# Summing the second layer of a top-1 expert network in 128 columns, with its banks, logits and key loads rearranged

## The chip, the cores and the metric

The kernel runs on one core of a Trainium2 chip. The metric is the device time of one execution in microseconds. Before the change three runs took 819.81, 827.26 and 831.77 us; their median is 827.26 us.

The core has a tensor engine (PE; its weight loads have a row of their own, PEld), a vector engine (DVE), a scalar engine (ACT), a general engine (POOL) and a sync engine (SP) that issues most transfers. Each engine works off its own instructions in the order in which they were written. Products land in PSUM, which has eight banks of 512 f32 columns on 128 partitions.

## The reference

Inputs are q, k and v (4 batches of 11,456 tokens, 128 channels), 49 agents per batch, and the weights of 8 experts with 1,024 hidden units.

```python
def sm(a, b):
    s = scale * (a @ b.transpose(0, 2, 1))
    s = s - s.max(-1, keepdims=True)
    e = np.exp(s)
    return e / (e.sum(-1, keepdims=True) + 1e-09)
a2k = sm(agents, k);  agent_v = a2k @ v
x = sm(q, agents) @ agent_v                       # 45,824 tokens of 128 channels
...
logits = x @ w_gate                               # 8 experts, the best one is taken
gate_w = softmax(logits)[best];  eom = 1 / (1 + exp(-(x @ w_output_gate)))
...
h = np.maximum(x[mask] @ w1[e], 0.0)              # for each expert e
out[mask] = gate_w[mask, None] * eom[mask, e, None] * (h @ w2[e])
```

## The kernel before

Every token is a mix of 49 agent averages, so the kernel keeps for each token the 49 exponentials of its scores instead of x. In f16 these stand three times in one row of 128: the rounded value, the rest that rounding lost, and 30 of the rounded values again. A DMA turns such rows, so that `x1` has the 128 numbers on partitions and the tokens in columns. For each batch the agent averages are multiplied into the first expert layer; only hidden units whose sign is not fixed for all tokens of the batch are kept (256 slots, `NBM` = 2 blocks of 128), and the others are added as one linear map `G`. Almost all tokens of a batch choose one expert; the tokens that do not ("left" tokens) are gathered and done again in 20 tiles with weights of their own.

The work of a batch, by the names of the code:

- **Keys and values.** `k_unit` and `v_unit` go over 12 units of 1,024 tokens (the last has 192). They give the agent averages. `folded` (line 869) then picks the expert, loads its two weight matrices and builds the first-layer weights `w` and `wr` (products `ha`, `hr`), the check weights `wc` (`hk`), the second-layer weights `vv` (`hv`) and the linear map `G` (`hg`). `wr` holds the 19 rows that did not fit into the 128 of `w`.
- **Queries.** `q_unit` and `q_rest` (line 1254) make scores, exponentials, the three-part f16 rows `e16`, the turned copy `x1`, a copy `x2` of its first 32 rows on partitions 32 to 63, then logits (`lg`) and the gate `smt`. `check` multiplies `x1` by `wc` (`ck`).
- **Tiles.** 92 tiles of up to 512 tokens. `mm1` (line 1443) makes the two blocks of the first layer in two banks: per block one product over 128 rows and one over the 19 rows of `wr`, block 0 from `x1` and block 1 from `x2`. `relu` writes the rounded `hh` on ACT and the rest `hl` on DVE. `mm2` (line 1476) makes the second layer for two groups of 128 tokens at a time, 256 columns each: `G` and then, for each block, `hh` times both halves of `vv` (256 columns) and `hl` times the first half. `finish` (line 1504) adds the two halves (ACT copies one, DVE adds the other), and `store` multiplies by the gate on POOL and stores.

**Banks.** `group` gives `mm1` of an even tile banks 0 and 1 and of an odd tile banks 2 and 3. The four others serve everything else: the halves of `y`, `ck`, `lg`, scores, averages and the fold.

**The order.** Nothing is scheduled by hand. A planner (`Clock`, `tick`, `block`, `idle`) runs while the program is written: it has a cost for each instruction (`Engine.cost`) and lets a waiting stream go on when its operands should be ready. `main_stream` (line 1548) chooses between `mm1` of the next tile and `mm2` of the oldest open tile. So a changed cost or rule moves instructions on every engine. All products below bear line 229, the line that emits an instruction.

**Left tiles.** They go in sets of 4, 4, 4, 3 (batches 0 and 1) and 3, 2 (batches 2 and 3). A set is prepared (`tbs`, `pbs`, gathers) only when the results of the set before the last one are stored; a tile then needs `let`, `lx`, 8 products `lh` and 8 products `ly` in f32 (two rows each in a trace).

Of the kernel before, what the change touches and what calls it, by code (L numbers as in the profile page):

```python
# [17 lines left out]
P = 128  # L18
# [14 lines left out]
YS = 2  # L33
# [10 lines left out]
G4 = 4  # L44
# [117 lines left out]
class Engine:  # L162
# [16 lines left out]
    def cost(self, op, ins, outs, k):  # L179
        n = _free(outs[0])  # L180
        if self.name == "PE":
            wide = ins[0].dtype == F32
            if op == "transpose":
                return 110.0 if wide else 58.0
            if not wide and ins[0].shape[0] <= 32:
                return n / 4.8 + 51.0
            if wide and _free(ins[0]) <= 64 and ins[0].shape[0] > 64 and n <= P:

                return max(58.0, n * 0.833 + 4.0) * min(1.0, _free(ins[0]) / 64.0 * 0.8)
            if wide and not self.clk.started and n <= P:  # L190
                return 221.0
            return max(157.0, n * 1.667 + 6.0) if wide else max(n, 50) / 2.4 + 2.5
        if "reduce" in op:
            n = _free(ins[0])
        if self.name == "ACT":
            return (51.0 if ins[0].name in self.clk.psum else 93.0) + n / 1.2 + 93.0 * (len(ins) - 1)
# [82 lines left out]
def agent_attention_top1_moe(ctx, tc, qT, kT, v, aT, wg, wo, w1, w2, cst, sides, slots, out):  # L279
# [53 lines left out]
    def group(i):  # L333
        return [NBM * (i % 2) + g for g in range(NBM)]
# [272 lines left out]
    def loads():  # L607
        for n, item in enumerate(ITEMS):
            while n >= FIRST_ITEMS and (picking[0] or not X1):
                yield None  # L610
# [3 lines left out]
            if n == 1:  # L614
                load_constants()

# [27 lines left out]

    def k_unit(b, u):
        if u == 0:
            K[b] = dict(
# [6 lines left out]
        spawn(k_rest(b, u, s, mark))  # L654
# [214 lines left out]
    def folded(b, ad):  # L869

        w1t, w2t = yield from choose(b, ad[:, 0:A], ad)
# [113 lines left out]
    def hidden(b, ad, w1t, w2t):  # L985
# [83 lines left out]
        for n in range(NB):  # L1069
            for k in range(NBM):  # L1070
                PE.matmul(o[32 * k:32 * k + 32, 0:P], ax[:, n, P:P + 32], sel[:, n, k * P:(k + 1) * P],
                          start=(n == 0), stop=(n == NB - 1))
        clk.vt["PE"] += TURN
        rest = wk.tile([P, P], F16, name=f"wr{b}", tag="w0")
        yield from DVE.q.tensor_copy(rest[0:32 * NBM], o[0:32 * NBM, 0:P])
# [165 lines left out]
    def q_unit(b, u):  # L1241
        s, mark = yield from scores(("q", b, u), f"qs{b}_{u}")
        spawn(q_rest(b, u, s, mark))

    rests = []

# [7 lines left out]
    def q_rest(b, u, s, mark):  # L1254
# [3 lines left out]
        while me > 3 and rests[me - 4] < 3 or me > 1 and not state.get(0, {}).get("w"):  # L1258
# [4 lines left out]
        z = wk.tile([P, 8, A2], F32, name=f"qz{b}_{u}", tag="qz", bufs=2)  # L1263
        yield from DVE.q.tensor_tensor(z[0:pp, 0:nt, 0:A], sv,
                          m[0:pp, 0:nt].unsqueeze(2).broadcast_to([pp, nt, A]), op=ALU.subtract)
        release(mark)
        ef = wk.tile([P, 8, A2], F32, name=f"ef{b}_{u}", tag="ef", bufs=5)
        ev = ef[0:pp, 0:nt, 0:A]
        yield from ACT.q.activation(ev, z[0:pp, 0:nt, 0:A], AF.Exp, scale=SCALE)
        yield from ACT.q.activation(z[0:pp, 0:nt, 0:A], ev, AF.Square)  # L1270
        while counted[0] < b - 1:
            yield None
        rank_, e2, d256 = (marks[b % 2][0][0:pp, k, 8 * u:8 * u + nt] for k in range(3))
        yield from DVE.q.tensor_reduce(e2, z[0:pp, 0:nt, 0:A], axis=AX.X, op=ALU.add)
# [3 lines left out]
        yield from POOL.q.tensor_copy(e16[0:pp, 0:nt, 2 * A:P], ev[:, :, AR:A])  # L1278
        while me > 0 and rests[me - 1] < 1:
# [6 lines left out]
        while vacant_turned() is None:  # L1286
            yield None
        x2 = place(("x2", b, u), vacant_turned()[1], [1024], F16)
        yield from SY.q.dma_start(x2[32:64, 0:nt * pp], x1[0:32, 0:nt * pp])
        X1[b, u] = x1, x2  # L1290
        spawn(check(b, u, x1), 1)
        rests[me] = 1
        while "gs" not in state.get(b, {}) or (me > 0 and rests[me - 1] < 2) \
                or me > 2 and rests[me - 3] < 3:
            yield None
        gs, s3 = state[b]["gs"], state[b]["s3"]
# [7 lines left out]
        def tl(nm, *sh):  # L1304
            return wk.tile([P, 8, *sh], F32, name=f"{nm}{b}_{u}", tag=nm, bufs=3)[0:pp, 0:nt]

        lv = lg[0:pp, 0:nt * 36].rearrange("p (t a) -> p t a", a=36)
        L = tl("lL", 16)
        yield from ACT.q.copy(L, lv[:, :, 18:34])
        yield from DVE.q.tensor_scalar(d256, lv[:, :, 16], 1e-9, None, op0=ALU.add)  # L1310
        yield from DVE.q.tensor_tensor(L, lv[:, :, 0:16], L, op=ALU.add)
        release(mark)
        rests[me] = 2
        while not clk.started:
            yield None
        rr = tl("rr")
        yield from DVE.q.tensor_scalar(rr, d256, s3[0:pp], None, op0=ALU.mult)
        yield from DVE.q.reciprocal(rr, rr)
        l = tl("ll", 16)
        yield from POOL.q.tensor_tensor(l, L, rr.unsqueeze(2).broadcast_to([pp, nt, 16]), op=ALU.mult)  # L1320
# [41 lines left out]
    def q_tail(b):  # L1362

        st = state[b]
        while "thr" not in st or not all((b, u) in checked for u in range(NU)):
# [46 lines left out]

    PRE = 6
    QU = 6

    MIX0 = [(2, 0)] + [(1, 0)] * 4 + [(0, 0)] + [(0, 2)] * 6
    MIX = [(3, 0)] * 4 + [(0, 0)] + [(0, 2)] * 6 + [(0, 0)]
# [6 lines left out]
    def small_products():  # L1424
        for kind, b, u in ITEMS:
            while kind == "q" and not roomy(NU * b + u, AHEAD):
# [14 lines left out]
    done, summed = set(), set()  # L1441

    def mm1(i):
# [4 lines left out]
        x1, x2 = (x[:, 512 * h:512 * h + w] for x in X1[b, u])  # L1448
# [13 lines left out]
        if 4 * h + n == UNITS[u][2]:  # L1462
            scored(("x2", b, u))
# [12 lines left out]
    def mm2(i, k, f):  # L1476
# [4 lines left out]
        if f == 0:  # L1481
            Y[i, k] = bank(f"y{i}_{k}"), hold()
            x1 = X1[b, u][0]
            for j in range(2):
                sl = slice(512 * h + (2 * k + j) * pp, 512 * h + (2 * k + j + 1) * pp)
                PE.matmul(Y[i, k][0][0:pp, j * 2 * C:(j + 1) * 2 * C], x1[:, sl], state[b]["G"].rearrange("p h c -> p (h c)"),
                          start=(j == 0), stop=False)
# [3 lines left out]
        for j in range(2):  # L1491
            y = Y[i, k][0][0:pp, j * 2 * C:(j + 1) * 2 * C]
            sl = slice((2 * k + j) * pp, (2 * k + j + 1) * pp)
            PE.matmul(y, hh[:, sl], vv[:, f].rearrange("p h c -> p (h c)"), start=False, stop=False)
            tick()
            PE.matmul(y[:, 0:C], hl[:, sl], vv[:, f, 0, :], start=False, stop=(f == NBM - 1 and j == 1))
            tick(0, 1)
        if f == NBM - 1:
            spawn(finish(i, k), 0)
            block()  # L1500

    OS = {}

    def finish(i, k):
        b, u, h, pp, n = tiles[i]
        if k == 0:
            while i > 3 and i - 4 not in done or i > 1 and i - 2 not in summed:
                yield None
            OS[i] = wk.tile([P, 4, C], F32, name=f"os{i}", tag="os", bufs=4)
        os = OS[i]  # L1510
        y, mark = Y.pop((i, k))
        yv = y.rearrange("p (j h c) -> p j h c", h=2, c=C)
        ol = wk.tile([P, 2, C], F32, name=f"ys{i}_{k}", tag="ys", bufs=YS)
# [554 lines left out]
```

## Time and profile before

| | |
|---|---|
| median of three runs | 827.26 us |
| the profiled execution | 834.87 us |
| its span, first to last instruction | 833.1 us |
| busy PE, DVE, ACT, POOL | 668.7, 549.3, 466.7, 370.0 us |
| first tile's first product / last second-layer product | 71.4 / 698.3 us |
| mean granted clock of PE | 0.904 |

The profiled execution is 0.9% above the median. A busy PE is not PE at its peak: a product counts as busy until its results have left, while the next one has long begun. "idle before" in a group of instructions is the engine's idle time just before them, with what ended it.

### The profile page before, as it was taken

To read this page: it belongs to the slowest core of one execution; us is meant where nothing else is said; L and a number is where in the kernel's file an instruction comes from. 1 tells how busy PE (TensorE), PEld (TensorE's weight loads), DVE (VectorE), ACT (ScalarE), POOL (GpSimd) and SP (SyncE) were. 2 spreads that over 40 slices of the span, in tenths; PEclk is the share of its full clock that TensorE was granted. 3 is DMA by queue.
4 is the path that set the end of the run, shared out by engine and by line. 5 is a ranking of instruction groups with operands and counts; after the bars stand their busy time and mean duration, and the time that the engine had idled before them with its cause. 6 is when DMAs were issued, how large, how long until landed. Compare 5 with 4: busy or idle time off the path is not lost. (4 is left out here: it accounts for less than half of the span.)

```text
span 833.1 us, 28225 instructions
## 1 busy us (share of the span) xinstructions
PE 668.7 (80%) x11198; PEld 511.7 (61%) x11198; DVE 549.3 (66%) x1881; ACT 466.7 (56%) x1316; POOL 370.0 (44%) x622
## 2 busy tenths in 40 slices
PE   9989778877787889778888988867989797386484
PEld 7776645655555656556656666645666577285374
DVE  2966547658886777679679888697878666324220
ACT  2445547674747667675776676537777763131131
POOL 1012415855343386634235768444456643431330
PEclk9999959999979999989999899668999999695787
DMA  8993773878656986965759748644644455352440
GB/s 325 354 285 90 182 195 93 253 189 249 177 174 159 240 230 146 261 201 145 219 113 272 204 132 249 217 110 117 149 134 128 140 188 154 123 177 70 145 165 6
DMA packets 106185, 149.11 MB, mean 179 GB/s; under 512 B 61272, under 2 KB 69642, under 8 KB 106048
## 3 DMA queue, kind: packets, MB, share of 16 engines
q1 hardware_dynamic: 104128, 145.02, 60.2%
q0 software_dynamic: 1920, 2.24, 1.3%
q8 instruction: 89, 1.46, 0.8%
q14 instruction: 48, 0.39, 0.2%
HBM read 97.51 MB, written 35.56 MB: 160 GB/s over the span
## 5 line engine op out<-in xcount | busy, mean ns | idle before, releaser
L229 PE MATMUL y<-vv,hh 128*128 128x256 f16 x720 | 163.4, 285 | 1.7 <-issue 1.7
L229 PEld LDWEIGHTS <-x_ld 128*128 128x128 f16 x1080 | 90.5, 103 | 108.8 <-issue 76.2
L229 PE MATMUL y<-vv,hl 128*128 128x128 f16 x720 | 144.5, 226 | 1.5 <-issue 1.1
L229 DVE SCALAR_TENSOR_TENSOR hl<-h,hh 128x512 f16<-128x512 f32 (+1 forms) x184 | 118.1, 668 | 37.7 <-ACT hh L229 33.6
L229 ACT ACTIVATE hh<-h 128x512 f16<-128x512 f32 (+1 forms) x184 | 98.6, 583 | 49.5 <-PE h L229 45.0
L229 PE MATMUL y<-gw,x_ld 128*128 128x256 f16 x360 | 80.3, 285 | 54.1 <-ACT ck L229 25.7
L229 ACT ACTIVATE ck<-ck 128x512 f32<-128x512 f32 x180 | 106.0, 589 | 31.6 <-PE ck L229 22.8
L229 POOL TENSOR_TENSOR os<-os,smt 128x512 f32<-128x512 f32 (+1 forms) x91 | 94.4, 1041 | 43.5 <-DVE os L229 30.5
L229 ACT COPY ys<-y 128x256 f32<-128x256 f32 x179 | 66.2, 371 | 60.3 <-PE y L229 56.1
L229 DVE TENSOR_TENSOR os<-y,ys 128x256 f32<-128x256 f32 x179 | 74.3, 416 | 37.7 <-ACT ys L229 33.2
L229 PE MATMUL ck<-wc,x_ld 128*128 128x256 f16 x360 | 76.3, 294 | 17.8 <-ACT ck L229 7.8
L229 PEld LDWEIGHTS <-hh 128*128 128x128 f16 x720 | 74.4, 103 | 15.1 <-issue 5.9
L229 PEld LDWEIGHTS <-hl 128*128 128x128 f16 x720 | 75.4, 105 | 5.6 <-DVE hl L229 0.8
L229 POOL TENSOR_TENSOR e<-ef,e 128x392 f16<-128x392 f32 (+1 forms) x48 | 42.7, 890 | 53.7 <-ACT e L229 52.8
L229 PE MATMUL h<-x_ld,w 128*128 128x512 f16 (+1 forms) x184 | 64.2, 392 | 0.7 <-DVE hl L229 0.7
L229 PE MATMUL qs<-at,q_ld 128*32 128x50 f32 (+1 forms) x2640 | 46.5, 213 | 11.2 <-issue 10.0
L229 PEld LDWEIGHTS qs<-at,q_ld 128*32 128x32 f32 (+1 forms) x2640 | 38.5, 113 | 22.5 <-issue 16.0
L229 PE MATMUL ks<-at,k_ld 128*32 128x50 f32 (+1 forms) x2188 | 49.5, 217 | 2.3 <-issue 1.5
L229 PEld LDWEIGHTS ks<-at,k_ld 128*32 128x32 f32 (+1 forms) x2188 | 42.6, 121 | 11.1 <-issue 7.5
L229 POOL TENSOR_TENSOR ev<-S,km_o 128x400 f32<-128x400 f32 (+1 forms) x36 | 32.8, 913 | 27.0 <-PE av L229 26.2
L229 ACT ACTIVATE lh<-lh 128x512 f32<-128x512 f32 x40 | 23.9, 597 | 35.5 <-PE lh L229 34.3
L229 ACT COPY S<-ks 128x400 f32<-128x400 f32 (+1 forms) x48 | 22.6, 471 | 34.5 <-PE ks L229 34.0
(349 smaller groups left out, 1507.4 us busy)
## 6 DMA issues: line engine op xcount, KB each, us to landing
v_ld<-v SPq DMA_DIRECT2D x44, 512.0 KB
q_ld<-qT SPq DMA_DIRECT2D x44, 512.0 KB
out<-os SPq DMA_DIRECT2D x88, 256.0 KB
k_ld<-kT SPq DMA_DIRECT2D x43, 512.0 KB
lws<-w SPq DMA_DIRECT2D x22, 512.0 KB
lw<-w SPq DMA_DIRECT2D x18, 512.0 KB
efd<-ef SPq DMA_DIRECT2D x44, 200.0 KB
x_ld<-x_ld SPq DMA_DIRECT2D x44, 64.0 KB
```

The source lines that it names most:

```text
L229: return getattr(self.eng, op)(*a, **k)
```

## The change

- **Second layer.** `mm2` sums both halves of the weights into the same 128 columns: two products of 128 columns with the same stationary operand in place of one of 256, for `G` and for `hh`. Four groups of tokens share one bank, so a tile has one bank for `y`, where it had two. `finish` reads it once: DVE multiplies by the gate if the gate is there when the planner gets to it, else ACT copies and POOL multiplies.
- **First layer.** `group` gives every tile banks 0 and 1. The others are six (`G4` = 2). `wr` lies on partitions 0 to 18 for both blocks, and `x2` and its 48 transfers are gone.
- **Logits.** Two products of 18 columns into one sum, where one of 36 columns was followed by an ACT copy and a DVE addition. The multiplication by `rr` moves from POOL to DVE.
- **Queries.** `q_rest` is cut into streams (`q_weights`, `q_squares`, `q_logits`, `q_gates`); up to six units may be under way before the gates (`DEEP`), four behind them (`GATES`).
- **Keys and values.** Loads and products of q and of k and v are two streams each. A batch's keys may begin once the tiles have come to six units ahead of the batch before it (`LEAD`, `reached`), and the fold waits until the tiles have come to the batch before.
- The planner's costs of products over 32 rows and of ACT with a sum are changed.

```diff
-G4 = 4
+G4 = 2
...
             if not wide and ins[0].shape[0] <= 32:
-                return n / 4.8 + 51.0
+                return n / 2.4 + 51.0 if n <= 64 else n / 2.4 + 2.5
...
     def group(i):
-        return [NBM * (i % 2) + g for g in range(NBM)]
+        return [g for g in range(NBM)]
...
     def loads():
-        for n, item in enumerate(ITEMS):
-            while n >= FIRST_ITEMS and (picking[0] or not X1):
-                yield None
+        for n, item in enumerate(ITEMS[:FIRST_ITEMS]):
...
+        spawn(later_loads("q", 3), -1)
+        spawn(later_loads("kv", 4), -1)
...
     def k_unit(b, u):
         if u == 0:
+            while b > 0 and "rec" not in K[b - 1] or not reached(NU * (b - 1) + LEAD):
+                yield None
...
     def folded(b, ad):
 
+        while not reached(NU * (b - 1)):
+            yield None
...
-        while me > 3 and rests[me - 4] < 3 or me > 1 and not state.get(0, {}).get("w"):
+        while me >= DEEP and (rests[me - DEEP] < 3 or rests[me - 4] < 1) or me > 1 and not state.get(0, {}).get("w"):
...
         for t in range(nt):
-            yield from PE.q.matmul(lg[0:pp, t * 36:(t + 1) * 36], x1[:, t * pp:(t + 1) * pp],
-                                   gs.rearrange("p k c -> p (k c)"), start=True, stop=True)
+            for k in range(2):
+                yield from PE.q.matmul(lg[0:pp, t * 18:(t + 1) * 18], x1[:, t * pp:(t + 1) * pp], gs[:, k, :],
+                                       start=(t == 0 and k == 0), stop=(t == nt - 1 and k == 1))
...
         for g in range(NBM):
-            rows = slice(32 * g, 32 * g + AR)
-            PE.matmul(p[g][0][:, 0:w], rest[rows, :], (x2 if g else x1)[rows, :], start=False, stop=True)
+            PE.matmul(p[g][0][:, 0:w], rest[0:AR, g * P:(g + 1) * P], x1[0:AR], start=False, stop=True)
...
-        for j in range(2):
-            y = Y[i, k][0][0:pp, j * 2 * C:(j + 1) * 2 * C]
-            sl = slice((2 * k + j) * pp, (2 * k + j + 1) * pp)
-            PE.matmul(y, hh[:, sl], vv[:, f].rearrange("p h c -> p (h c)"), start=False, stop=False)
+        for j in range(2 * k, 2 * k + 2):
+            y = Y[i][0][0:pp, j * C:(j + 1) * C]
+            sl = slice(j * pp, (j + 1) * pp)
+            PE.matmul(y, hh[:, sl], vv[:, f, 0, :], start=False, stop=False)
+            PE.matmul(y, hh[:, sl], vv[:, f, 1, :], start=False, stop=False)
             tick()
-            PE.matmul(y[:, 0:C], hl[:, sl], vv[:, f, 0, :], start=False, stop=(f == NBM - 1 and j == 1))
+            PE.matmul(y, hl[:, sl], vv[:, f, 0, :], start=False, stop=(f == NBM - 1 and j == n - 1))
...
-        yield from ACT.q.copy(ol[0:pp], yv[0:pp, :, 1, :])
-        yield from DVE.q.tensor_tensor(os[0:pp, 2 * k:2 * k + 2, :], yv[0:pp, :, 0, :], ol[0:pp], op=ALU.add)
-        release(mark)
...
+        if (b, u) in SM and clk.ready[SM[b, u].name] <= max(clk.vt["DVE"], clk.now()):
+            yield from DVE.q.tensor_tensor(o, yv, gate(), op=ALU.mult)
+            release(mark)
+        else:
+            yield from ACT.q.copy(o, yv)
+            release(mark)
             while (b, u) not in SM:
                 yield None
+            yield from POOL.q.tensor_tensor(o, o, gate(), op=ALU.mult)
```

Of the 92 tiles of the changed program 72 take the ACT copy and 20 the DVE multiplication.

Three places on PE show how the order moves. The first is the start of the second layer of tile 40 (`y40`; `x11_8` is the turned copy of its unit, `gw_1` its linear map). Before:

```order
L229 LDWEIGHTS x11_8_ld_6802
L229 MATMUL y40_0_7432<-gw_1_85,x11_8_ld_6802 128x256
L229 LDWEIGHTS x11_8_ld_6802
L229 MATMUL y40_0_7432<-gw_1_85,x11_8_ld_6802 128x256
L229 LDWEIGHTS hh40_0_7284
L229 MATMUL y40_0_7432<-vv1_4829,hh40_0_7284 128x256
L229 LDWEIGHTS hl40_0_7285
L229 MATMUL y40_0_7432<-vv1_4829,hl40_0_7285 128x128
```

In the changed program the same tile's products of `hh` and `hl`, with a logit product among them:

```order
L229 LDWEIGHTS hh40_0_7989
L229 MATMUL y40_8100<-vv1_5194,hh40_0_7989 128x128
L229 LDWEIGHTS hh40_0_7989
L229 MATMUL y40_8100<-vv1_5194,hh40_0_7989 128x128
L229 LDWEIGHTS x11_9_ld_7471
L229 MATMUL lg1_9_7856<-gs_1_102,x11_9_ld_7471 128x18
L229 LDWEIGHTS hl40_0_7990
L229 MATMUL y40_8100<-vv1_5194,hl40_0_7990 128x128
```

The product of 256 columns has become two of 128, each with a weight load of its own.

The second place is the first product of the linear map of batch 3 (`hg3`), whose tiles begin with tile 69. Before:

```order
L229 LDWEIGHTS w3_11593
L229 MATMUL h72_1_11806<-x13_1_ld_11277,w3_11593 128x512
L229 LDWEIGHTS wr3_11629
L229 MATMUL h72_0_11802<-x13_1_ld_11277,wr3_11629 128x512
L229 LDWEIGHTS wr3_11629
L229 MATMUL h72_1_11806<-x23_1_ld_11350,wr3_11629 128x512
L229 MATMUL hg3_11820<-w2t3_11085,al3_11668 128x128 x3
```

In the changed program:

```order
L229 LDWEIGHTS wr2_7942
L229 MATMUL h66_1_11858<-x12_10_ld_11259,wr2_7942 128x512
L229 LDWEIGHTS x13_0_ld_11661
L229 MATMUL ck3_0_1_11853<-wc3_11730,x13_0_ld_11661 128x256
L229 LDWEIGHTS x13_0_ld_11661
L229 MATMUL ck3_0_1_11853<-wc3_11730,x13_0_ld_11661 128x256
L229 MATMUL qs3_2_11857<-at_76,q3_2_ld_11228 32x50 x32
L229 LDWEIGHTS x13_0_ld_11661
L229 MATMUL ck3_0_2_11913<-wc3_11730,x13_0_ld_11661 128x256
L229 LDWEIGHTS x13_0_ld_11661
L229 MATMUL ck3_0_2_11913<-wc3_11730,x13_0_ld_11661 128x256
L229 MATMUL hg3_11863<-w2t3_10642,al3_11742 128x128
```

It stood behind tile 72, the fourth tile of the new batch, and now stands behind tile 66, two tiles before the batch begins.

The third place is the table product of the third set of left tiles (`tbs0_8`); `y91` is the last tile. Before:

```order
L229 MATMUL y89_0_14007<-vv3_11559,hl89_1_13835 128x128
L229 LDWEIGHTS x13_10_ld_13455
L229 MATMUL y89_1_14036<-gw_1_85,x13_10_ld_13455 128x256
L229 MATMUL tbs0_8_14027<-big0_2_13966,ones_90 128x32
L229 LDWEIGHTS x13_10_ld_13455
L229 MATMUL y89_1_14036<-gw_1_85,x13_10_ld_13455 128x256
```

In the changed program:

```order
L229 LDWEIGHTS hl91_1_14626
L229 MATMUL y91_14748<-vv3_11538,hl91_1_14626 96x128
L229 MATMUL let0_4_14771<-kc_71,big0_1_13059 98x128
L229 MATMUL tbs0_8_14775<-big0_2_14721,ones_90 128x32
L229 MATMUL lx0_4_14777<-let_sb0_4_14773,lav0_10765 128x128
L229 MATMUL lh0_4_0_14796<-lxs0_4_14781,lws0_4_14694 128x128 x3
```

It moved from the middle of tile 89 to behind the last product of the second layer; four left tiles (0 to 3) are complete there, where five were.

## Rows read from the trace of the kernel before

**Rows 1.** The page's first part: busy us (share of the span) xinstructions

```profile
PE 668.7 (80%) x11198; PEld 511.7 (61%) x11198; DVE 549.3 (66%) x1881; ACT 466.7 (56%) x1316; POOL 370.0 (44%) x622
```

**Rows 2.** Busy time by stretch: main stage, tail, opening, and two batch boundaries

```profile
core 0: us, PE busy (x) PEld busy (x) DVE busy (x) ACT busy (x) POOL busy (x), PEclk, DMA share, GB/s
...
71.40:698.30 626.90, 518.76 (x9633) 379.89 (x9631) 468.19 (x1574) 410.14 (x1177) 318.23 (x546) 0.92 0.65 178
698.30:833.10 134.80, 82.68 (x543) 75.81 (x542) 37.04 (x174) 31.79 (x79) 41.14 (x45) 0.78 0.40 127
100.80:118.60 17.80, 11.10 (x199) 6.50 (x199) 5.57 (x14) 7.43 (x20) 4.15 (x7) 0.58 0.84 204
...
387.90:407.30 19.40, 16.23 (x397) 12.21 (x397) 15.45 (x51) 9.97 (x28) 8.69 (x17) 1.00 1.04 293
542.00:577.00 35.00, 21.78 (x288) 14.15 (x277) 31.61 (x126) 15.79 (x43) 15.22 (x30) 0.77 0.43 117
```

**Rows 3.** The same view for instructions on `y` alone: PE, DVE, ACT

```profile
554.10:577.20 23.10, 0.02 (x1) 0.41 (x1) 0.37 (x1) 0.80 0.35 95
```

**Rows 4.** Groups by shape: xcount | busy us, mean ns | idle before, by releaser

```profile
L229 ACT ACTIVATE ck<-ck 128x512 f32<-128x512 f32 x176 | 103.7, 589 | 31.2 <-PE ck L229 22.6 <-DVE a L229 1.6 <-DVE qm L229 0.9
...
L229 PE MATMUL y<-gw,x_ld 128*128 128x256 f16 x352 | 78.3, 284 | 51.7 <-ACT ck L229 25.7 <-DVE os L229 11.6 <-DVE avs L229 4.6
L229 PE MATMUL ck<-wc,x_ld 128*128 128x256 f16 x352 | 74.3, 293 | 17.1 <-ACT ck L229 7.8 <-ACT gsq L229 3.2 <-DVE qz L229 1.3
L229 DVE TENSOR_TENSOR os<-y,ys 128x256 f32<-128x256 f32 x176 | 73.1, 416 | 37.7 <-ACT ys L229 33.2 <-ACT ck L229 2.1 <-DMA out<-os 0.6
L229 PEld LDWEIGHTS <-hl 128*128 128x128 f16 x704 | 73.1, 104 | 5.6 <-DVE hl L229 0.8 <-issue 0.6
...
L229 ACT COPY ys<-y 128x256 f32<-128x256 f32 x176 | 65.0, 371 | 56.7 <-PE y L229 52.5 <-DVE os L229 2.3 <-DVE a L229 0.6
```

**Rows 5.** Waits of PE: engine tile <- releaser: us in total, times, longest us

```profile
PE y L229 <- ACT ck L229: 25.7, 34, 1.9
```

**Rows 6.** PE's timeline: start us, us, instructions; second-layer products in a row

```profile
595.27 0.27 PE L229 MATMUL y<-vv,hh 128*128 128x256 f16 x1
595.38 0.22 PE L229 MATMUL y<-vv,hl 128*128 128x128 f16 x1
595.43 0.27 PE L229 MATMUL y<-vv,hh 128*128 128x256 f16 x1
```

**Rows 7.** PE's timeline: a pair over 16 rows; a tile's first layer and what follows

```profile
596.49 0.48 PE L229 MATMUL pbs<-pptsb,big 16*128 16x128 f32 x2
...
675.12 0.38 PE L229 MATMUL h<-x_ld,w 128*128 128x512 f16 x1
675.43 0.39 PE L229 MATMUL h<-x_ld,wr 19*128 19x512 f16 x2
675.75 0.28 PE L229 MATMUL y<-gw,x_ld 128*128 128x256 f16 x1
675.87 0.39 PE L229 MATMUL lh<-lxs,lw 128*128 128x128 f32 x2
```

**Rows 8.** PE's timeline: the logit products of one unit

```profile
183.16 0.36 PE L229 MATMUL lg<-gs,x_ld 128*128 128x36 f16 x8
```

**Rows 9.** Timelines of ACT and DVE behind the first layer of rows 7

```profile
675.85 1.08 ACT L229 ACTIVATE hh<-h 128x512 f16<-128x512 f32 x2 [0.33 <-PE h L229]
...
676.48 1.29 DVE L229 SCALAR_TENSOR_TENSOR hl<-h,hh 128x512 f16<-128x512 f32 x2 [0.37 <-ACT hh L229]
```

**Rows 10.** PE's timeline: left tiles around the last second-layer product

```profile
688.48 0.41 PE L229 MATMUL tbs<-big,ones 128*128 128x32 f32 x2 [1.90 <-DVE big L229]
...
702.54 0.39 PE L229 MATMUL lx<-let_sb,lav 98*128 98x128 f32 x2
...
707.22 0.39 PE L229 MATMUL lx<-let_sb,lav 98*128 98x128 f32 x2
...
720.42 0.62 PE L229 MATMUL tbs<-big,ones 128*128 128x24 f32 x2 [7.99 <-DVE big L229]
```

More of the change, by code (lines that the diff above doesn't have):

```diff
@@ L615, in loads, with later_loads @@
                 load_constants()
+        spawn(later_loads("q", 3), -1)
+        spawn(later_loads("kv", 4), -1)
+    def later_loads(kinds, most):
+        for item in ITEMS[FIRST_ITEMS:]:
+            if item[0] not in kinds:
+                continue
+            while picking[0] or not X1 or sum(x[0] in kinds for x in held) >= most or not vacant():
+                yield None
+            yield from load(item)
     def scores(item, name):
@@ L869, in folded @@
     def folded(b, ad):
+        while not reached(NU * (b - 1)):
+            yield None
         w1t, w2t = yield from choose(b, ad[:, 0:A], ad)
@@ L1262, in q_rest, with q_weights @@
         yield from DVE.q.tensor_reduce(m[0:pp, 0:nt], sv, axis=AX.X, op=ALU.max)
-        z = wk.tile([P, 8, A2], F32, name=f"qz{b}_{u}", tag="qz", bufs=2)
-        yield from DVE.q.tensor_tensor(z[0:pp, 0:nt, 0:A], sv,
-                          m[0:pp, 0:nt].unsqueeze(2).broadcast_to([pp, nt, A]), op=ALU.subtract)
+        ef = wk.tile([P, 8, A2], F32, name=f"ef{b}_{u}", tag="ef", bufs=DEEP + 1)
+        ev = ef[0:pp, 0:nt, 0:A]
+        yield from DVE.q.tensor_tensor(ev, sv, m[0:pp, 0:nt].unsqueeze(2).broadcast_to([pp, nt, A]), op=ALU.subtract)
         release(mark)
-        ef = wk.tile([P, 8, A2], F32, name=f"ef{b}_{u}", tag="ef", bufs=5)
+        spawn(q_weights(b, u, me, ef))
+    def q_weights(b, u, me, ef):
+        base, pp, nt = UNITS[u]
         ev = ef[0:pp, 0:nt, 0:A]
[L1269 to L1274, printed above, removed]
+        yield from ACT.q.activation(ev, ev, AF.Exp, scale=SCALE)
         e16 = e16s[(NU * b + u) % 4]
@@ L1285, in q_rest @@
                                   transpose=True)
[L1286 to L1290, printed above, removed]
+        X1[b, u] = x1
         spawn(check(b, u, x1), 1)
@@ L1311, in q_rest, with q_squares @@
-        yield from DVE.q.tensor_tensor(L, lv[:, :, 0:16], L, op=ALU.add)
+            for k in range(2):
+                yield from PE.q.matmul(lg[0:pp, t * 18:(t + 1) * 18], x1[:, t * pp:(t + 1) * pp], gs[:, k, :],
+                                       start=(t == 0 and k == 0), stop=(t == nt - 1 and k == 1))
+        spawn(q_logits(b, u, me, ef, lg, mark), 1)
+    def q_squares(b, u, ev):
+        base, pp, nt = UNITS[u]
+        while counted[0] < b - 1 or len(squared) < NU * b + u:
+            yield None
+        z = wk.tile([P, 8, A2], F32, name=f"qz{b}_{u}", tag="qz", bufs=2)
+        yield from ACT.q.activation(z[0:pp, 0:nt, 0:A], ev, AF.Square)
+        e2 = marks[b % 2][0][0:pp, 1, 8 * u:8 * u + nt]
+        yield from DVE.q.tensor_reduce(e2, z[0:pp, 0:nt, 0:A], axis=AX.X, op=ALU.add)
+        squared.add((b, u))
@@ L1364, in q_tail @@
         st = state[b]
-        while "thr" not in st or not all((b, u) in checked for u in range(NU)):
+        while "thr" not in st or not all((b, u) in checked and (b, u) in squared for u in range(NU)):
             yield None
@@ L1440, in agent_attention_top1_moe @@
     Y = {}
-    done, summed = set(), set()
+    done = set()
     def mm1(i):
```

133 lines of the change are left out of this document (66 added, 67 removed).

## The prediction

> **What bounds the kernel now.** I read the page's busy times first. PE is busy 80% of the span, DVE 66%, ACT 56%, POOL 44% [rows 1]: no engine is full, so shares alone don't tell. Next come the busy times by stretch. The kernel has an opening up to 71.4 us, which hardly changes here, a main stage of 92 tiles up to 698.3 us, and a tail of left tiles [rows 2]. In the main stage PE is busy 518.76 of 626.9 us; the other 108 us are waits. [...]
>
> Then the groups by shape, for what PE waited for. Of its 108 idle us, 51.7 lie just before the `G` products that open a half of `y`, and 17.1 before `ck` [rows 4]. They were ended by ACT (`ck`), DVE (`os`, `avs`): by readers that free a bank. The other products of `y` hardly wait. So the main stage is bound by PE together with the turnover of the four banks that `y`, `ck`, logits, scores and averages share. Last, the stretches without second-layer work: 101 to 119 us (clock 0.58), 388 to 407 us, and 554 to 577 us, where one single product of `y` stands [rows 2, 3]. There the next queries or the next batch's fold are late.
>
> The idle column understates a wait, since a product counts as busy until its results have left: a 256-column product has a row of 284 ns [rows 4], while the next starts after 109 ns (595.27 to 595.38) [rows 6]. One of them shows 0.76 us on average (25.7 us in 34 waits [rows 5]), so 68.8 us are about 90 waits; 0.175 us more for each is 16 us: about 85 us in all.
>
> **The change part by part**, against the profiled execution's 834.9 us.
>
> *Waits for banks.* By the tile counts, 180 halves of `y`, 180 of `ck` and some 180 others (logits, scores, averages, sums of v) turned over four banks, 135 each; now 92 `y`, and the rest as before, turn over six, 75 each. Each `y` is freed by one reader instead of two: before, ACT 371 ns and then DVE 416 ns [rows 4]; now one read of 512 columns, about 0.6 us by the `ck` row's 589 ns. I take 70% of the 85 us as gone: -60 us. The ends are -35 (ACT and DVE were late for other reasons) and -85 (all).
>
> *Work of ACT, DVE and POOL.* ACT loses 176 copies (65.0 us [rows 4]) and gains 72 of about 589 ns (42 us); DVE loses 176 additions (73.1 us [rows 4]) and gains 20 multiplications of some 650 ns (13 us; two reads of 512 columns took 1.29 us [rows 9]); POOL loses 20 of its 92 gate multiplications and 48 small ones. None of them ends a stage by itself, so I cost this at nothing; PE's work covers it, and what it brings is in the waits.
>
> *The stretches without second layer.* In the changed order the map of batch 3 stands two tiles before that batch instead of four tiles into it, that of batch 2 likewise before its batch, while that of batch 1 stays where it was relative to its tiles. The two later gaps should close. Their idle time is 19.4 - 16.23 = 3.2 us and 35 - 21.78 = 13.2 us, and at a clock of 0.77 about half of the second gap ran at the lower level, which cost its busy time some 5 us [rows 2]: 21 us, of which I take -18 (ends -8 and -25). The opening stretch has 6.7 us idle and a clock of 0.58; now units 2 and 3 are scored before the first tile, and tile 4 stands behind `y1` instead of `y3`: -8 (ends 0 and -17).
>
> *Rest products of the first layer.* Before, block 0 and block 1 lie on different rows of the array and run at once: the pair takes 0.39 us, as one does, and the next product starts 0.32 us after it [rows 7]. On the same rows they follow each other, which costs at least the 0.21 us that 512 columns take, twice the 109 ns of 256 [rows 6] (the other end is 0.31, if the second load is not hidden). The nearest row is a pair over 16 rows of one place: 0.48 us, against 0.39 us for a pair over all 128 [rows 7], so a load of about 0.1 us shows. 92 tiles x 0.21 to 0.31 = 20 to 29: +25. [...]
>
> *Logits.* Eight products in 0.36 us, the last lasting 0.185, are 25 ns apart [rows 8]. With 18 columns I take the same 25 ns, as the load remains: 360 more are +9 (lower end 0).
>
> *Split pairs.* 1,080 products of 256 columns (109 ns apart) become 2,160 of 128 columns. The 128-column `hl` product, whose load and whose successor's load are both there, is followed after 55 ns [rows 6]: 2 x 55 = 110, so +1.
>
> *Two banks for the first layer.* Before, the next tile had the other pair. In [rows 7, 9] the rest products start at 675.43 and DVE is done at 676.48 + 1.29 = 677.77: the chain is 2.34 us, the first block's bank free after some 1.7. I counted PE's products between one tile's first layer and the next in the changed order, at the spacings of [rows 6 to 8]: 39 of 91 stretches are under 2.5 us, only a dozen under 1.5. +10 (ends +5 and +25, if DVE is often late).
>
> *Tail.* PE does one left tile less in the main stage, 4.7 us (702.54 to 707.22 [rows 10]): -5. In the tail it is one more, and the third set's table product starts after the last `y` instead of 9.8 us before it (688.48 [rows 10]); each such product has waited for DVE, once 7.99 us [rows 10]. A set's start passes on to the next, so I add the 9.8: +5 net (ends +3 and +11). The 48 transfers saved wait for nothing that shows: 0.
>
> Sum: -60 - 18 - 8 + 25 + 9 + 1 + 10 + 5 = -36, or 799 us of the profiled execution's 834.9. That execution is 0.9% above the median of the runs; brought to the median (x 827.26 / 834.87) it is 792 us.
>
> **Rivals.**
>
> *The waits are late readers, not scarce banks.* PE waits for `ck`'s reader because ACT's queue is late, and two more banks shift the wait. For: 25.7 us are ended by `ck` alone [rows 4], whose read stays. Against: ACT is busy 410 of 627 us [rows 2], so it catches up. With -35 for banks, -8 for the gaps and 0 for the opening stretch: -43 + 50 = +7, 842 of the profiled execution, 834 at the median: no change. Chance 0.17.
>
> *Two banks are too few.* Each short stretch waits a microsecond for DVE, 39 x 1 us instead of 10: 828, at the median 820: within 2%. For: DVE is busy 75% of the main stage (468 of 627) [rows 2]. Against: it loses 60 us of work. Chance 0.08.
>
> *Slower: the split products pay for their loads.* The load of 128 columns has a row of 104 ns [rows 4], twice the spacing of 55 ns. If in a row of 128-column products the load is no longer hidden, the 1,080 added products cost 104 - 55 = 49 ns each, 53 us, and all 2,160 106 us: 852 to 905, at the median 844 to 897. If the added ones alone pay, the forecast's gain is gone at 88 ns a product (36 us over 1,080 is 33, on top of 55), and it is slower by 2% at 104 ns. Against: `hl` products follow at 55 ns and logits at 25 ns with a load each [rows 6, 8]. Chance 0.10. [...]
>
> **How the numbers follow.** The forecast has 0.65. About 2% is what a measurement of this kernel can tell from no change: 810.7 to 843.8 us. All low ends of its terms at once give 730 at the median, all high ends 859; half-way to either is 761 to 825, the forecast's own range, and 0.60 of its 0.65 is faster by over 2%. The first two rivals fall within 2% nearly wholly: 0.05 + 0.17 + 0.08, less 0.02 that is faster or slower, is 0.28. Slower is 0.10 + 0.01, faster 0.60 + 0.01. The range of 755 to 835 takes in the forecast and the first two rivals and leaves out the third and the far ends.
>
> **What would show it.** Right: idle before `y<-gw` under 20 us where it was 51.7; products of `y` near 55 ns apart; no stretch of 20 us without `y` after 300 us; the main stage at about 580 us, the tail about 10 us longer. Wrong: `h` products waiting for DVE `hl` for over 25 us in all; 80 ns or more between the two products of one `hh`; idle before `y` that remains, with ACT as its end; over 0.65 us from the first rest product to whatever follows the second; a third set of left tiles that starts much later than 10 us after the last `y`.

## The result and the profile after

The changed kernel took 785.59 us (median of four runs, 775.39 to 792.13), beside 828.68 us of the kernel before on the same chip: a ratio of 0.942 [0.927, 0.957]. The ratio compares the runs that lie within 1.5% of their kernel's fastest (two of the four runs of the changed kernel, 783.39 and 775.39). The forecast was 792 us. The profiled execution took 792.13 us, 0.8% above its median, where the sum of the terms had come to 799.

The page's first part, busy us (share of the span) and instructions, answers to [rows 1]:

```profile
PE 676.0 (86%) x12807; PEld 541.3 (68%) x12807; DVE 497.1 (63%) x1720; ACT 436.4 (55%) x1159; POOL 329.9 (42%) x555
```

Busy time by stretch, with the columns of [rows 2]: main stage, tail, and the stretch of the opening in which PE had been held up.

```profile
75.10:645.90 570.80, 513.07 (x11134) 398.25 (x11132) 412.73 (x1400) 376.74 (x1016) 278.87 (x478) 0.95 0.69 188
645.90:790.40 144.50, 90.94 (x597) 83.39 (x596) 39.76 (x188) 34.40 (x85) 41.49 (x45) 0.78 0.38 125
101.00:119.00 18.00, 17.63 (x492) 14.18 (x494) 13.19 (x43) 15.75 (x47) 8.80 (x17) 1.00 0.81 220
```

Read the lengths first: the main stage lost 56 us (626.9 to 570.8), the tail gained 9.7, and the first tile starts 3.7 us later (75.1 instead of 71.4). PE is as busy there as before, within 6 us, so nearly all of the gain was idle time. The mean granted clock rose from 0.92 to 0.95; the clock records of both traces have two levels, 1.0 and 0.5, and the main stage had 95.6 us at 0.5 before and has 54.6 now.

The groups of PE, with the columns of [rows 4]:

```profile
L229 PE MATMUL y<-vv,hh 128*128 128x128 f16 (+1 forms) x1440 | 168.2, 224 | 2.1 <-issue 1.4 <-ACT hh L229 0.5
...
L229 PE MATMUL y<-gw,x_ld 128*128 128x128 f16 x720 | 82.5, 224 | 10.5 <-ACT ck L229 3.0 <-DVE avs L229 2.1 <-issue 1.5
L229 PE MATMUL ck<-wc,x_ld 128*128 128x256 f16 (+1 forms) x360 | 73.1, 283 | 6.7 <-DMA x_ld<-e 2.2 <-DVE avs L229 1.8 <-ACT ck L229 1.5
L229 PE MATMUL lg<-gs,x_ld 128*128 128x18 f16 x720 | 63.7, 174 | 3.8 <-ACT os L229 2.3 <-DMA x_ld<-e 1.4
L229 PE MATMUL h<-x_ld,w 128*128 128x512 f16 (+1 forms) x184 | 61.9, 382 | 1.3 <-DVE hl L229 1.1
```

The idle time before the `G` products of a `y` fell from 51.7 to 10.5 us, that before `ck` from 17.1 to 6.7. (The rows after count all tiles; with the last tiles' shapes the values before are 54.1 and 17.8.) `h` waits for DVE 1.1 us in all. What is new stands in the waits of PE (us in total, times, longest) whose end is "issue", that is, no event that the trace holds:

```profile
PE av L229 <- issue: 12.1, 6, 3.0
PE ks L229 <- issue: 10.3, 5, 3.9
...
PE y L229 <- issue: 6.5, 7, 1.7
...
PE qs L229 <- issue: 3.2, 3, 2.0
```

They are 21 waits and 32.1 us, all in the main stage. In the main stage of the kernel before the same view had these, 15.5 us (18.4 with its tail):

```profile
PE qs L229 <- issue: 10.0, 8, 4.5
...
PE y L229 <- issue: 2.9, 4, 1.2
...
PE ks L229 <- issue: 1.5, 2, 0.9
...
PE hg L229 <- issue: 1.1, 1, 1.1
```

PE's timeline answers to [rows 6 to 8]: second-layer products with two logits between them, and a tile's rest products.

```profile
600.25 0.60 PE L229 MATMUL h<-x_ld,wr 19*128 19x512 f16 x2
600.78 0.21 PE L229 MATMUL lg<-gs,x_ld 128*128 128x18 f16 x2
...
601.97 0.20 PE L229 MATMUL lg<-gs,x_ld 128*128 128x18 f16 x2
602.02 0.22 PE L229 MATMUL y<-vv,hl 128*128 128x128 f16 x1
602.08 0.27 PE L229 MATMUL y<-vv,hh 128*128 128x128 f16 x2
602.19 0.22 PE L229 MATMUL y<-vv,hl 128*128 128x128 f16 x1
602.25 0.27 PE L229 MATMUL y<-vv,hh 128*128 128x128 f16 x2
```

Two `hh` products take 0.11 us from their start to that of the next (602.08 to 602.19), an `hl` 0.06, two logits 0.05, and the rest pair 0.53 (600.25 to 600.78) where it was 0.32.

The last `y` starts at 645.68 and the third set's table at 649.07, 3.4 us behind it; here are that product and the next set's:

```profile
649.07 0.38 PE L229 MATMUL tbs<-big,ones 128*128 128x32 f32 x2 [3.06 <-DVE big L229]
...
679.98 0.62 PE L229 MATMUL tbs<-big,ones 128*128 128x24 f32 x2 [7.92 <-DVE big L229]
```

### The profile page after: what moved, and what is told of

It is laid out like the page before. It is cut to its first block, busy times and chain, and to the rows that moved or that the text cites. A ratio compares the mean times of both kernels' runs of the same rounds, so it can differ in the third digit from the quotient of the medians.

```text
span 790.4 us, 30955 instructions
## 1 busy us (share of the span) xinstructions
PE 676.0 (86%) x12807; PEld 541.3 (68%) x12807; DVE 497.1 (63%) x1720; ACT 436.4 (55%) x1159; POOL 329.9 (42%) x555
## 3 DMA queue, kind: packets, MB, share of 16 engines
q8 instruction: 101, 1.65, 0.9%
## 5 line engine op out<-in xcount | busy, mean ns | idle before, releaser
L229 PE MATMUL y<-vv,hh 128*128 128x128 f16 (+1 forms) x1440 | 168.2, 224 | 2.1 <-issue 1.4
L229 PEld LDWEIGHTS <-x_ld 128*128 128x128 f16 (+1 forms) x1800 | 127.1, 102 | 56.0 <-issue 40.2
L229 DVE SCALAR_TENSOR_TENSOR hl<-h,hh 128x512 f16<-128x512 f32 (+1 forms) x184 | 120.4, 669 | 55.3 <-ACT hh L229 54.6
L229 ACT ACTIVATE ck<-ck 128x512 f32<-128x512 f32 (+1 forms) x180 | 106.4, 592 | 28.6 <-PE ck L229 27.2
L229 PEld LDWEIGHTS <-hh 128*128 128x128 f16 (+1 forms) x1440 | 111.5, 101 | 10.8 <-issue 7.4
L229 PE MATMUL y<-gw,x_ld 128*128 128x128 f16 x720 | 82.5, 224 | 10.5 <-ACT ck L229 3.0
L229 PE MATMUL ck<-wc,x_ld 128*128 128x256 f16 (+1 forms) x360 | 73.1, 283 | 6.7 <-DMA x_ld<-e 2.2
L229 PE MATMUL lg<-gs,x_ld 128*128 128x18 f16 x720 | 63.7, 174 | 3.8 <-ACT os L229 2.3
L229 ACT COPY os<-y 128x512 f32<-128x512 f32 (+1 forms) x72 | 41.2, 574 | 29.4 <-PE y L229 17.1
L229 PE MATMUL h<-x_ld,wr 19*128 19x512 f16 (+1 forms) x184 | 55.4, 381 | 0.0
L229 PE MATMUL av<-ev,v_ld 128*32 128x50 f32 (+2 forms) x2152 | 35.0, 216 | 12.1 <-issue 12.1
```

Of the source, the lines that this page charges most:

```text
L229: return getattr(self.eng, op)(*a, **k)
```

## The experiments

Each edit starts from the changed kernel, except where its heading names the kernel before; the planner then writes the whole order anew. Ratios are to the kernel before, run on the same chip.

**Four shared banks instead of six.**

```diff
-            others[:] = range(G4, 8)
+            others[:] = range(G4, 6)
```

> The changed kernel, except that the tiles' stage shares four banks (2 to 5) where it shared six; banks 6 and 7 stay unused there. First-layer banks, second layer, pace and logits as changed. Theory (scarce banks): some 450 turnovers over four banks are 113 each; before they were 135 each with about 85 us of waits, in the changed kernel 75 each with about 22, so the waits rise by about 40: idle before y<-gw and ck back to 35 to 50 us in all (17 in the changed kernel), time 810 to 825 us. Rival 1 (late readers, banks do not matter): idle within 5 us of the changed kernel's, time 780 to 792 us. Rival 2 (one read per y frees banks so early that four are enough): the same numbers as rival 1, but then with ACT's read of y no longer among the ends of the idle.

It took 846.61 us, ratio 1.017 [1.012, 1.023]: taken out of the changed kernel, the two banks are worth some 60 us, all of the gain and more. Rivals 1 and 2 fall. But the theory expected 810 to 825 us, and it had the place half wrong. Here are the groups, and then two stretches of the same kernel for instructions on `y` alone (length; PE, DVE, ACT; clock, DMA share, GB/s):

```profile
L229 PE MATMUL y<-gw,x_ld 128*128 128x128 f16 x720 | 81.6, 223 | 22.9 <-ACT ck L229 10.0 <-DVE os L229 3.8 <-ACT os L229 2.6
L229 PE MATMUL ck<-wc,x_ld 128*128 128x256 f16 x360 | 70.7, 279 | 7.6 <-ACT os L229 4.9 <-ACT ck L229 1.3 <-DVE ll L229 0.6
```

```profile
198.30:292.80 94.50, 0.01 (x1) 0.00 (x0) 0.37 (x1) 0.70 0.69 205
547.60:588.40 40.80, 0.00 (x0) 0.66 (x1) 0.37 (x1) 0.71 0.51 132
```

The direct waits before `y` and `ck` came back by only 13 us. The rest shows in two stretches of 95 and 41 us without second layer, at clocks of 0.70 and 0.71, where the changed kernel has a single one of 31.5 us (229.7 to 261.2). In the first, the tiles of batch 0 are through at 198 us (at 230 in the changed kernel), but the last averages (`av`) of batch 1 come at 215 (at 181 there), and its fold takes some 70 us in either kernel. So with four banks the tiles ran ahead while the small products that the next batch needs came later. That they came late for want of a bank is argued from this order; no view shows which bank each of them waited for.

**A second pair of first-layer banks, four shared.**

```diff
-G4 = 2
+G4 = 4
...
-        return [g for g in range(NBM)]
+        return [NBM * (i % 2) + g for g in range(NBM)]
```

> The changed kernel, except that the first layer alternates between two pairs of banks again and four banks are shared. Against the run with four shared banks and one pair it prices the second pair alone. Theory (one pair costs 10 us or less; h products waited 1.3 us for DVE hl in the changed kernel): within 10 us of that run, 800 to 825 us. Rival (the single pair is what slows the planner's order down, beyond the waits at h): 15 us or more below that run, 800 us or less.

849.48 us, ratio 1.021 [1.015, 1.027]. The second pair is worth nothing (2.9 us slower than without it, less than the spread of either): the theory is right on the difference, and its level of 800 to 825 us is wrong, as in the run before.

**The old pace of loads, keys and values.**

```diff
...
-            while b > 0 and "rec" not in K[b - 1] or not reached(NU * (b - 1) + LEAD):
-                yield None
...
-        while not reached(NU * (b - 1)):
-            yield None
...
-    spawn(small_products("q"), 4)
-    spawn(small_products("kv"), 4)
+    spawn(small_products(), 4)
```

> The changed kernel with loads and small products of q, k and v in one stream again, in the old mix, and without the waits that tie a batch's keys and its fold to the tiles. Theory (closing the two later gaps and shortening the opening one was worth 26 us): 800 to 815 us, with stretches of 15 us or more without second-layer products before batch 2 or batch 3. Rival 1 (the gaps were short of banks, which six banks cure): 780 to 792 us, no such stretch. Rival 2 (the pace made the main part of the gain): 820 us or more.

801.65 us, ratio 0.964 [0.961, 0.968]; beside the changed kernel's 785.59, and 788.14 when run again, the pace is worth 13 to 16 us, and the stretches without `y` before batches 2 and 3 are back (31.5 and 30.4 us). The theory holds, but at half the size. The view by stretch tells why: main stage and tail.

```profile
70.20:674.00 603.80, 530.18 (x11372) 409.22 (x11371) 440.50 (x1455) 368.38 (x996) 251.84 (x450) 0.93 0.67 184
674.00:795.20 121.20, 76.60 (x500) 70.08 (x499) 32.80 (x163) 28.83 (x71) 35.92 (x40) 0.77 0.40 124
```

The main stage is 33 us longer, the tail 23 us shorter. No left tile ran in the two gaps; this is the same view for the product `lx` alone (PE, PEld, ACT), two of which every left tile has:

```profile
379.80:411.30 31.50, 0.00 (x0) 0.00 (x0) 0.00 (x0) 0.84 0.65 175
528.00:558.40 30.40, 0.00 (x0) 0.00 (x0) 0.00 (x0) 0.83 0.43 130
70.20:674.00 603.80, 3.08 (x14) 2.11 (x14) 1.84 (x7) 0.93 0.67 184
```

The left tiles begin at about the same time in both (570 us here, 578 in the changed kernel). So seven of them stand ahead of the last `y` of this longer main stage, where the changed kernel has four, and the tail has three fewer left to do.

**Rest products on two row groups, with `x2`.**

```diff
...
-            PE.matmul(p[g][0][:, 0:w], rest[0:AR, g * P:(g + 1) * P], x1[0:AR], start=False, stop=True)
+            rows = slice(32 * g, 32 * g + AR)
+            PE.matmul(p[g][0][:, 0:w], rest[rows, :], (x2 if g else x1)[rows, :], start=False, stop=True)
...
```

> The changed kernel with the rest products of the two blocks on different rows of the array again, with the second copy x2 and its 48 transfers (and three buffers for one small tile of the fold, where there were two). Theory (PE bounds the stage and the serial pair costs 92 x 0.21 us = 19 us): 765 to 772 us, from one rest product to the next 3 ns, not 226. Rival 1 (the serial pair lies beside waits that stay): 780 to 790 us. Rival 2 (the copy comes late and the transfers crowd the others): 790 us or more, with first-layer products that wait for a DMA.

784.64 us (772.87 to 787.17, beside 832.14 of the kernel before; no interval). The two products of a pair start 3 ns apart again, and PE is busy 16.7 us less in the main stage, but the time is not clear of the changed kernel's 785.59 (775.39 to 792.13). So the theory falls, and rival 1 has the time. The main stage is only 8.2 us shorter:

```profile
74.10:636.70 562.60, 496.42 (x10961) 396.90 (x10959) 420.85 (x1390) 379.74 (x1023) 281.31 (x479) 0.95 0.70 193
636.70:782.20 145.50, 91.30 (x597) 83.63 (x597) 39.74 (x193) 34.59 (x86) 47.05 (x51) 0.78 0.40 134
```

**Logits in 36 columns.**

```diff
-            for k in range(2):
-                yield from PE.q.matmul(lg[0:pp, t * 18:(t + 1) * 18], x1[:, t * pp:(t + 1) * pp], gs[:, k, :],
-                                       start=(t == 0 and k == 0), stop=(t == nt - 1 and k == 1))
+            yield from PE.q.matmul(lg[0:pp, t * 36:(t + 1) * 36], x1[:, t * pp:(t + 1) * pp],
+                                   gs.rearrange("p k c -> p (k c)"), start=True, stop=True)
...
```

> The changed kernel with logits of 36 columns again: 8 products a unit instead of 16, then an ACT copy and a DVE addition, and the multiplication by rr on POOL. Theory (PE bounds the stage; 360 products at 25 ns are 9 us): 776 to 782 us, the changed kernel having taken 785.59. Rival 1 (the bank of the logits is held longer and ACT and DVE get 96 more instructions): 788 us or more, with more idle before y<-gw. Rival 2 (the 9 us lie beside waits or move into other ones): 783 to 788 us.

801.59 us, ratio 0.966 [0.960, 0.972]: slower by 13 to 16 us than the changed kernel, as rival 1 has it by the time. The idle time before `y<-gw` hardly grew (12.5 us, where it was 10.5), that before `ck` rose from 6.7 to 11.8. So the 360 more products pay for themselves here. How much of the 13 to 16 us is the bank that comes free later, and how much the order alone, stays open (see the nudges).

**The second layer in 256 columns.** `mm2`, `finish` and `store` are those of the kernel before.

```diff
...
-            PE.matmul(y, hh[:, sl], vv[:, f, 0, :], start=False, stop=False)
-            PE.matmul(y, hh[:, sl], vv[:, f, 1, :], start=False, stop=False)
+            PE.matmul(y, hh[:, sl], vv[:, f].rearrange("p h c -> p (h c)"), start=False, stop=False)
...
-        yield from DVE.q.tensor_tensor(o, yv, gate(), op=ALU.mult)
+        yield from ACT.q.copy(ol[0:pp], yv[0:pp, :, 1, :])
+        yield from DVE.q.tensor_tensor(os[0:pp, 2 * k:2 * k + 2, :], yv[0:pp, :, 0, :], ol[0:pp], op=ALU.add)
```

> The changed kernel with the second layer as before the change: two banks a tile, 256 columns with two halves, an ACT copy and a DVE addition for each half (four buffers for the copies, where there were two, and the second half waits for the first one's tile). Six banks stay shared. Turnovers: 540 over six banks are 90 each, where the changed kernel has 75 and the kernel before 135; on the line through 22 us of waits at 75 and 85 us at 135 that is 38 us. Theory (the 128-column sum is worth what it saves in banks): 795 to 810 us. Rival 1 (six banks alone do it, the sum is worth nothing; 1,080 fewer products need less code): 775 to 790 us. Rival 2 (the single read of y is the main part of the gain): 820 us or more.

823.81 us, ratio 0.990 [0.982, 0.997]: rival 2 by the time. The group shows the second reader, DVE `os`, as the first of the ends:

```profile
L230 PE MATMUL y<-gw,x_ld 128*128 128x256 f16 x360 | 79.4, 281 | 37.4 <-DVE os L230 14.8 <-ACT ck L230 9.5 <-DVE ef L230 4.9
```

The span of the profiled execution is 32 us longer than the changed kernel's. Of these only 13 are in the main stage (584.1 us); the tail is 163.7 us, 19 longer, as the first left tile begins at 630 us, not 578. So the time has the size of rival 2, but most of it does not lie where `y` is read, and why the left tiles begin later stays open.

**The kernel before with six shared banks and nothing else.**

```diff
-G4 = 4
+G4 = 2
...
-        return [NBM * (i % 2) + g for g in range(NBM)]
+        return [g for g in range(NBM)]
...
```

> The kernel before with two first-layer banks for every tile and six shared banks, and nothing else of the change (four buffers for the copies of y, and the second half of y waits for the first one's tile). Turnovers per shared bank fall from 135 to 90. Theory (the banks are the gain; waits of 85 us fall to about 38, two first-layer banks cost 5 to 10): 785 to 800 us. Rival 1 (late readers): 820 us or more. Rival 2 (with the old pace the gaps before batches 2 and 3 stay, and the tiles only reach them earlier): 805 to 820 us, with stretches of 15 us or more without second-layer products.

810.27 us, ratio 0.977 [0.971, 0.983]: rival 2. The idle before `y` falls to 19.9 us and that before `ck` to 12.7, 39 us less together over all tiles (54.1 and 17.8 before), for 18 us of time. Rest products now wait 12.0 us for the copy `x2`, and the stretches without `y` remain (32.2 and 41.2 us). The parts need each other: the banks alone give 2.3%, the whole change without them (the first run) loses 1.7%.

**Scores and averages in 64-column pieces.**

```diff
-    PART, TURN = 32, 100.0
+    PART, TURN = 64, 100.0
...
-            part[0] = 2 * PART
+            part[0] = PART
```

> The changed kernel with scores and averages always in pieces of 64 columns, where most were of 32: about half of their 6,900 products. In the changed kernel's trace PE pauses 18 times, 29.6 us in all, with nothing to wait for, and each pause ends 1.3 to 1.5 us after a 16 KB block of its instructions has landed. Theory (those pauses are code that comes too late, because such small products are used up faster than their code is loaded): blocks of code 101 to about 75 or 80, pauses under 15 us. Of the time: 64 columns took 66 ns per 128 against 52 for 32-column pieces in the kernel before, 1,700 groups of 128 cost 24 us more, so 780 to 792 us in all. Rival (the pauses are waits for something else that the trace does not show, such as a late transfer): pauses stay at 25 us or more and the time is 800 us or more.

767.38 us, ratio 0.929 [0.923, 0.935], the pauses gone: no wait of PE that ends with "issue" is left. This is the page's row of the code queue, first of the changed kernel (packets, MB, share of 16 engines):

```profile
q8 instruction: 101, 1.65, 0.9%
```

and of this one, with its main stage and tail:

```profile
q8 instruction: 78, 1.28, 0.7%
```

```profile
75.60:628.50 552.90, 526.41 (x8205) 415.12 (x8202) 418.62 (x1405) 376.02 (x1016) 274.90 (x475) 0.97 0.71 195
628.50:764.00 135.50, 84.42 (x575) 77.39 (x574) 40.08 (x186) 33.37 (x82) 42.03 (x45) 0.78 0.39 127
```

The theory holds, and the time is better than either side expected, although a group of 128 columns takes some 60 to 65 ns in such pieces and 48 to 52 in the changed kernel's 32-column ones.

**The changed kernel again, and two nudges of the planner.**

```diff
-    AFTER = {"PE": 190.0, "ACT": 220.0, "DVE": 180.0, "POOL": 170.0, "SP": 0.0}
+    AFTER = {"PE": 190.0, "ACT": 225.0, "DVE": 180.0, "POOL": 170.0, "SP": 0.0}
```

The second nudge makes the 190.0 of PE 195.0.

> The changed kernel unedited, as the measure for the edits of this call and the earlier ones. Expected: 780 to 792 us by its earlier runs (775.39 to 792.13).

> The changed kernel with one number of the planner's model moved by 5 ns (how long an ACT result takes to be seen, 220 to 225). The instructions are the same work; only their order moves. It asks how much an order alone is worth, since every one-part edit moves the order too. Theory (part of the 16 us by which the kernels with the old pace and with 36-column logits were slower is the order alone): within 12 us of the changed kernel, 774 to 798 us, but not within 2. Rival (orders of the same work take the same time): within 3 us.

> As the other nudge, with another number: how long a PE result takes to be seen, 190 to 195 ns. Same theories: 774 to 798 us and not within 2 us of the changed kernel, or within 3 us.

788.14 us unedited (ratio 0.951 [0.941, 0.960]), 790.06 (0.951 [0.940, 0.963]) and 797.14 (0.958 [0.948, 0.969]) with the nudges. These are main stage and tail of the first nudge, and then of the unedited kernel:

```profile
75.10:663.70 588.60, 528.02 (x11413) 408.47 (x11412) 430.21 (x1441) 374.53 (x1014) 271.64 (x466) 0.95 0.68 186
663.70:787.10 123.40, 76.68 (x515) 70.11 (x513) 32.65 (x162) 29.25 (x72) 38.77 (x42) 0.79 0.38 126
```

```profile
75.60:644.80 569.20, 514.34 (x11134) 399.44 (x11132) 417.50 (x1400) 376.56 (x1016) 278.39 (x478) 0.95 0.69 188
644.80:787.90 143.10, 92.75 (x597) 84.94 (x596) 39.14 (x189) 34.39 (x85) 41.93 (x45) 0.77 0.39 126
```

5 ns in the model move the main stage by 19 us and the end by almost nothing; the other nudge moves the end by 9. The work is not quite the same, either: the planner cuts scores and averages into larger pieces where PE would be idle, so PE has 13,003 and 12,910 products with the nudges and 12,807 without. The first nudge doesn't separate theory from rival (1.9 us), the second speaks for the theory, though the intervals overlap. So a one-part edit prices a part only to some 10 us.

**64-column pieces and the rest products on two row groups.** Both edits above together.

> The changed kernel with scores and averages in pieces of 64 columns, which took 767.38 us without pauses for code, and with the rest products on two row groups and the copy x2, which alone changed nothing (784.64). Theory (with the pauses gone PE's own work sets the main stage, so the 19 us that the pair takes off it count now): 750 to 760 us, the main stage 535 to 545 us where it was 552.9. Rival 1 (the copies and their waits cost what the pair saves, as before): 764 to 772 us. Rival 2 (the left tiles set the end, whatever the main stage does): the main stage shorter by 10 us or more and the tail longer by as much.

758.16 us, ratio 0.914 [0.907, 0.922], the fastest. The time lies in the theory's range, but the main stage is far below the theory's 535 to 545 us and the tail longer, so the mechanism is rival 2's:

```profile
73.20:589.70 516.50, 484.72 (x8082) 393.72 (x8080) 404.79 (x1364) 371.44 (x1003) 272.03 (x467) 0.97 0.75 205
589.70:757.70 168.00, 109.58 (x722) 100.40 (x721) 48.88 (x221) 41.60 (x102) 55.90 (x60) 0.79 0.41 129
```

The main stage is 36 us shorter than with the 64-column pieces alone and the tail 32 us longer. The first left tile starts at 583 us, six us before the last `y`, and from there the left tiles take 174 us, with hardly anything else for PE to do. This is the third set's table, 24 us after the last `y` (589.44), waiting for DVE:

```profile
613.11 0.64 PE L229 MATMUL tbs<-big,ones 128*128 128x32 f32 x2 [5.54 <-DVE big L229]
```

## Why the prediction was right, point by point

- **Waits for banks: -60.** Right in the size of the waits, and the banks are the cause, but the way from waits to time was partly luck. The idle time before `y<-gw` and `ck` fell from 68.8 to 17.2 us, and at 0.175 us more for each of some 68 waits that vanished (90 at first, 51.6 of 68.8 gone) that is -64. Taking the two banks away costs 58 to 61 us, so that the waits were late readers alone (first rival) is refuted. But the term took a microsecond of waits for one of time, and the runs do not: with four banks 13 us of these waits came back for some 60 us of time, and six banks alone took 39 us of them for 18 us. What I had not seen is that the averages of the next batch, and its fold behind them, come later when banks are few: in the run with four, the loss is mostly there.
- **Later gaps: -18; opening: -8.** After 300 us no stretch of 20 us without `y` is left, and the one of 101 to 119 us runs at a clock of 1.00 with PE busy for 17.63 of 18 us. (The lower level of the first term is the 0.5 of the clock records: of the 35 us of the second gap 15.8 ran at it before.) The one stretch that is left, 31.5 us before batch 1, I had not counted as closing. But the first tile comes 3.7 us later, and undoing the pace costs 13 to 16 us where the two terms have 26: 33 us of main stage, of which the tail gives 23 back. I had priced the main stage alone and not the left tiles, which begin at about the same time either way: in a longer main stage more of them stand ahead of the last `y`.
- **Rest products: +25.** From its first product to its successor the pair takes 0.53 us where it took 0.32, so 92 x 0.21 = 19; the lower end was right, and the 16-row pair was the wrong row to lean on. The two loads here have the same rows, and the second product starts 0.226 us after the first, little over the 0.21 us that the prediction took for 512 columns, so at most 0.02 us of the second load shows.
- **Logits: +9, split pairs: +1.** Two logits take 0.05 us and two `hh` products 0.11, so the third rival (loads that show, 88 ns a product and more) never came up. What undoing the logits cost, 13 to 16 us, says that the price on PE is not the price of the change.
- **Two first-layer banks: +10.** Too high: `h` waits 1.1 us for DVE, and a second pair is worth nothing. So the short stretches that I counted cost almost nothing; the second rival falls.
- **Tail: +5 net.** The third set's table stood 9.8 us before the last `y` and now stands 3.2 behind its end (649.07 after 645.90), and the tail grew by 9.7 us, as the term had it. From the table to the end it is 144.6 us before and 141.3 after, so the shift of 13.0 us came through but for 3.3.
- **Left out: +17.** The pauses that end with "issue" grew from 15.5 to 32.1 us in the main stage. I had counted 1,080 and 360 more products by their columns and not by their code. By and large the pauses of the runs go with their blocks of code. Over the whole span they are 18.4 us at 89 blocks (kernel before), 19.5 at 93 (256 columns), 27.1 at 98 (36-column logits), 32.1 at 101 and none at 78 (64-column pieces), though 29.3 at 96 (four banks). Against it stand the waits and the clock, which fell less often: in the main stage 9 times where it was 14, and the lower level lasted 41 us less. How the remaining gain divides between clock and gaps is not settled, since neither was changed alone.

The main stage came to 571 us for the 580 forecast. The terms that erred had errors of either sign, 6 to 17 us each, so that the sum came within 7 us is partly luck.

## What to carry to other kernels

When several streams share a few PSUM banks, count turnovers per bank and readers per turnover before anything that PE computes: here two banks were worth some 60 us, while 19 us less of PE's own work won nothing clear of the spread, and once the pauses for code were gone 9 us, which an order alone can move as well. Ask of every added product what its code costs, too. Price a gain by when the kernel ends, not by when one of its stages does. Where an end stage has a chain of its own, time won ahead of it comes back as a longer tail unless the chain starts earlier.

## What the runs showed of the hardware

Code is loaded while the kernel runs: the code queue of the changed kernel has 101 blocks of 16 KB, 1.65 MB in all. That PE can use it up faster than it comes is read from the pauses and the landings of the blocks. This is PE's timeline in the changed kernel, in the middle of a group of 64 products on one tile of `v`:

```profile
290.06 0.74 PE L229 MATMUL av<-ev,v_ld 128*32 128x50 f32 x47
293.81 0.39 PE L229 MATMUL av<-ev,v_ld 128*32 128x50 f32 x17 [3.01 <-issue]
```

The same stretch by engine, with the columns of [rows 2]; the DMA engines are full in it (1.05):

```profile
290.80:293.80 3.00, 0.00 (x0) 0.00 (x0) 0.47 (x1) 1.07 (x3) 0.39 (x1) 1.00 1.05 361
```

The 48th product has the operands and the bank of the 47th, so there was nothing to wait for, yet PE stood for 3.01 us. By the records of the code queue a block landed 1.39 us before it went on, and all 21 pauses, 32.1 us, ended 1.3 to 1.5 us after a block. (The expectation of the 64-column run has 18 of them with 29.6 us.) Small products that follow each other after 7 ns, or 12 on average, are where it strikes most: 25.6 of the 32.1 us lie before `av`, `ks` and `qs`. Full DMA engines are not the condition: in the pause of 2.0 us that ends at 168.32 us their share is 0.70. The blocks go with PE's products: 101 for 12,807 here and 89 for 11,198 in the kernel before, one to some 127 and 126.
